# First batch by head pairs over seven PSUM banks, batch 1's q turned by TensorE, and transfers planned on one resource, in a fused attention and MLP-mixer kernel

## The chip, the cores and the metric

The kernel runs on one core of one Trainium2 chip. The metric is device time in microseconds (us). Some single runs of the kernel before fell over 1.5% above the fastest; they stand in medians and ranges, but not in ratios. A profile is one execution, and its span (first to last instruction) is some 2 us shorter than the time of the same run.

Engines: PE is TensorE (PEld its weight loads), DVE is VectorE, ACT is ScalarE, POOL is GpSimd, SP is SyncE. SPq is SP's queue, which issues the DMA transposes. POOL issues the loads. L765 is line 765 of the kernel's file; the change shifts lines, so the up products are L765 before and L779 after, the down products L859 and L874.

## The reference, cut to what matters

```python
k_proj = einsum('ks,bhsd->bhkd', E, k);  v_proj = einsum('ks,bhsd->bhkd', F, v)   # 1024 rows -> 64
attn   = softmax(q @ k_proj^T / 8)                                                # 8 batches, 8 heads, 1024 x 64
x      = (attn @ v_proj), heads side by side                                      # 1024 x 512 per batch
u      = x + (relu(x^T @ w_tok1) @ w_tok2)^T                                      # token mixing
out    = u + relu(u @ w_ch1) @ w_ch2                                              # 512 -> 1536 -> 512
```

## The kernel before

The channel product is done by a Strassen-like scheme (seven products of quarters instead of eight, for "up" and "down"). Per batch the order is: project k and v, transpose the projected k, scores, exp, attend, token mixing (all called the *front*), then u must be transposed before the up products of its two halves (j = 2b and 2b+1) can start. For batch 0 TensorE transposes u; for batches 1 to 7 a DMA transpose does it.

No engine's order is written by hand. Each piece is a job with an engine, an estimated duration and a deadline. A list scheduler in the kernel's own Python orders all jobs once, and the program is emitted and pinned in that order: **each engine's instructions stand in the planned order, whatever the real times are**.

```python
pl = Planner({"U": 3, "D": 3, "F": 2})            # banks a stream may hold; F (front) lives in banks 6 and 7
def sp(t, fn, **kw): return pl.add("SP", t, t + 2.0, fn, **kw)      # transposes and stores
def ld(mb, fn, **kw):                                               # loads: a resource of their own
    t = mb / 0.40
    return pl.add("LD", t, t + 2.0, fn, **kw)
# ... buffers that matter below
qT   = tile_of([P, H, NJ, P], BF16, "qT")
uT_t = [tile_of([P, NJ, DMC, P], BF16, f"uT{i}") for i in range(2)]   # transposed u, one per half
g21_t = [tile_of([P, 2, 2 * P], BF16, f"g21{i}") for i in range(2)]
# ... end of token2(b, si): u is turned by DMA once four row blocks are there
sp(4.0, lambda: nc.sync.dma_start_transpose(
        out=uT_t[i].rearrange("p s dc q -> p (s dc) q"),
        in_=u_t[b % 2][:, i * NJ : (i + 1) * NJ].rearrange("p s d -> p (s d)")), ...)
# ... VectorE sums of quarters of u^T, needed by four of the seven up products
def s_sums(j):
    one(0, a21, a22, add=True); one(2, a11, a21); one(1, St[:, 0], a11, deps=(0,)); one(3, a12, St[:, 1], deps=(1,))
```

The softmax here doesn't subtract the row's maximum and nothing guards it: scores larger than these inputs give would overflow.

## Time and profile before

| | |
|---|---|
| time, median of 3 runs | 475.3 us (473.65 to 480.99, the last slow) |
| span of the profiled run | 471.6 us |
| TensorE columns of the whole program, counted at 2.4 per ns | 404.3 us |
| lost against that | 67.3 us |

The "loss" is my main ruler. I add up the columns of all matmuls in the program's order (a 128x256 matmul has 256) and divide by 2400 per us: the time at which an instruction would start if TensorE never waited and took columns at that rate throughout. The trace gives when it did start; the difference is the loss up to there. The 2400 is a convention of the ruler. At a granted clock of 1.00 the trace of the kernel before has one 128x256 matmul 109 ns after the other (median, 208 to 364 us), about 2350 columns per us.

| batch whose k/v projection starts | 1 | 2 | 3 | 4 | 7 | end |
|---|---|---|---|---|---|---|
| trace, us | 57.5 | 92.8 | 152.2 | 204.1 | 360.7 | 471.6 |
| loss, us | 34.0 | 37.3 | 48.7 | 50.8 | 58.2 | 67.3 |

Three sources can be read off: 34 us in the start, 11.4 us between batches 2 and 3, and 2.2 to 2.6 us in each later batch.

Before, busy time by stretch. Columns: stretch, its length, then busy us of PE, PEld, DVE, ACT, POOL with instruction counts, granted TensorE clock, mean busy share of the DMA engines, GB/s.

```profile
core 0: us, PE busy (x) PEld busy (x) DVE busy (x) ACT busy (x) POOL busy (x), PEclk, DMA share, GB/s
0.00:52.00 52.00, 33.72 (x302) 23.25 (x304) 28.32 (x81) 13.30 (x30) 23.80 (x38) 0.74 1.17 186
104.00:156.00 52.00, 42.79 (x346) 32.91 (x348) 34.04 (x83) 23.03 (x43) 9.21 (x10) 0.93 0.67 124
208.00:260.00 52.00, 50.08 (x430) 40.02 (x432) 38.48 (x93) 28.64 (x52) 11.43 (x13) 1.00 0.72 142
```

In the first stretch TensorE is idle for a third of the time and its clock is 0.74 on average; in 104 to 156 us it is idle for 9 us; later it is nearly always busy.

Before, waits (engine and line, what was waited for: us in total, times, longest us):

```profile
PE ps L765 <- DMA uT<-u: 8.5, 1, 8.5
PE ps L464 <- DVE kp L443: 7.6, 9, 1.3
PE ps L522 <- DVE x_sb L562: 5.0, 8, 1.8
```

One single wait of 8.5 us is the largest. Before, timelines of PE, SP's queue and POOL around it (start us, us, engine, line, operation, output and input, count, idle time before and what ended it):

```profile
48.56 0.60 PE L765 MATMUL ps<-uT,wc_sb 128*128 128x256 bf16 x4
...
55.98 28.91 SPq L487 DMA_TRANSPOSE qT<-q_sb  x4
...
95.94 1.53 POOL L297 DMA_DIRECT2D k_sb<-in_k_dram  x2 [4.20 <-PE ps L596]
97.45 1.50 POOL L297 DMA_DIRECT2D v_sb<-in_v_dram  x2
...
100.52 14.79 SPq L616 DMA_TRANSPOSE uT<-u  x2
...
115.56 1.01 PE L765 MATMUL ps<-uT,wc_sb 128*128 128x256 bf16 x4 [8.49 <-DMA uT<-u]
```

The first up product starts at 48.56 us. Batch 1's transposes of u are issued from 100.52 us, just behind four loads of k and v, and the first lands 15.0 us after its issue (the chain of waits has it as one piece); 4.2 us is the shortest landing in this trace. TensorE, which has run out of batch 0's work, waits.

### The profile page before, as it was taken

What the parts mean: (1) busy time and instruction counts of PE and PEld (TensorE: products, weight loads), DVE (VectorE), ACT (ScalarE), POOL (GpSimd) and SP (SyncE); (2) the same over time, 40 slices, a digit from 0 to 9 for tenths busy, and PEclk for the clock granted to TensorE, in tenths of its full rate; (3) what the DMA queues carried; (4) which work ended last, traced back from release to release, by engine and by line L of the source; (5) the groups of instructions that cost most, each with busy time, mean ns of one, the idle gap of its engine ahead of it and who ended that gap; (6) DMA issues with size and microseconds to landing.
All of it is one profiled execution on the core that took longest, in us unless ns stands there. A gap on an engine that the chain in (4) does not pass through costs nothing.

```text
span 471.6 us, 9198 instructions
## 1 busy us (share of the span) xinstructions
PE 424.9 (90%) x3665; PEld 338.9 (72%) x3692; DVE 326.7 (69%) x784; ACT 235.3 (50%) x428; POOL 107.2 (23%) x122
## 2 busy tenths in 40 slices
PE   4757889992999989999999999999999999999994
PEld 2526768771877777878777877877777887888883
DVE  2476768681878787786957786876957796766561
ACT  1321567522563665457543764457444764455541
POOL 8541031321101412031212221040101020112112
PEclk8576999997999999999999999999999999999999
DMA  8999999979393896649742998359522402241222
GB/s 125 207 199 207 189 195 196 164 151 178 89 169 56 152 209 130 135 66 217 169 133 46 194 192 145 98 82 215 107 91 46 133 4 89 47 81 55 90 89 91
DMA packets 93675, 61.68 MB, mean 131 GB/s; under 512 B 59840, under 2 KB 89024, under 8 KB 93632
## 3 DMA queue, kind: packets, MB, share of 16 engines
q0 software_dynamic: 30784, 29.63, 40.1%
q1 hardware_dynamic: 62848, 31.46, 28.0%
q8 instruction: 29, 0.48, 0.4%
q14 instruction: 14, 0.11, 0.1%
HBM read 59.24 MB, written 16.78 MB: 161 GB/s over the span
## 4 chain that ended last, share of the span: by engine, by line
PE 63%; DVE 16%; DMA 13%; ACT 3%; issue 2%; POOL 2%; DVEq 0%; POOLq 0%; ACTq 0%
PE ps L765 23%; PE ps L859 22%; DMA uT<-u 11%; PE ps L576 5%; PE ps L596 4%; DVE S L635 3%; DVE G L799 3%; DVE x_sb L562 2%; DMA q_sb<-in_q_dram 2%; PE ps L545 2%; PE ps L427 2%; PE ps L522 2%; PE ps L653 1%; DVE G L746 1%; DVE u L607 1%
## 5 line engine op out<-in xcount | busy, mean ns | idle before, releaser
L859 PEld LDWEIGHTS <-G 128*128 128x128 bf16 x1344 | 130.8, 98 | 22.0 <-issue 1.8
L859 PE MATMUL ps<-wc_sb,G 128*128 128x256 bf16 x768 | 104.5, 273 | 1.2 <-DVE da L907 1.1
L765 PEld LDWEIGHTS <-wc_sb 128*128 128x128 bf16 x768 | 72.8, 98 | 28.4 <-issue 12.5
L786 ACT ACTIVATE G<-ps 128x512 bf16<-128x512 f32 x96 | 57.4, 597 | 62.5 <-PE ps L765 62.0
L859 PE MATMUL ps<-wT,G 128*128 128x256 bf16 x576 | 78.1, 273 | 0.1
L765 PE MATMUL ps<-uT,wc_sb 128*128 128x256 bf16 x384 | 58.0, 274 | 8.8 <-DMA uT<-u 8.5
L765 PEld LDWEIGHTS <-wT 128*128 128x128 bf16 x576 | 55.4, 98 | 14.5 <-issue 4.5
L891 POOL TENSOR_TENSOR o<-o,u 128x512 f32<-128x512 f32 x32 | 37.4, 1168 | 104.3 <-ACT o L889 104.3
L891 POOL TENSOR_TENSOR db<-db,u 128x512 f32<-128x512 f32 x16 | 19.0, 1188 | 183.6 <-ACT db L889 183.6
L765 PE MATMUL ps<-S,wc_sb 128*128 128x256 bf16 x384 | 57.6, 273 | 1.3 <-ACT ua L792 1.0
L765 PE MATMUL ps<-S,wT 128*128 128x256 bf16 x384 | 54.9, 274 | 0.0
L746 DVE CUSTOM_DVE_ANT_0 g<-ps,ub 128x512 bf16<-128x512 f32 x48 | 32.8, 684 | 30.6 <-PE ps L765 30.5
L562 DVE TENSOR_TENSOR x_sb<-ps,rdn 128x256 bf16<-128x256 f32 x128 | 50.8, 415 | 0.9
L531 ACT ACTIVATE a<-ps 128x512 bf16<-128x512 f32 x64 | 37.8, 599 | 24.9 <-PE ps L522 24.8
L792 ACT COPY ua<-ps 128x512 f32<-128x512 f32 x48 | 28.2, 587 | 38.7 <-PE ps L765 38.6
L607 DVE TENSOR_TENSOR u<-ps,x_sb 128x512 bf16<-128x512 f32 x56 | 38.0, 685 | 12.6 <-PE ps L596 12.4
L799 DVE TENSOR_TENSOR G<-G 128x512 bf16<-128x512 bf16 x96 | 44.1, 459 | 3.3
L746 DVE CUSTOM_DVE_ANT_0 G<-ps,ua 128x512 bf16<-128x512 f32 x48 | 32.8, 683 | 12.5 <-ACT ua L792 12.3
L545 PE MATMUL ps<-vb,a 128*128 128x130 bf16 x256 | 34.0, 226 | 6.2 <-DVE x_sb L562 4.7
L545 PEld LDWEIGHTS <-a 128*128 128x128 bf16 x256 | 23.5, 100 | 17.4 <-issue 10.3
L805 ACT COPY ps<-ps 128x512 f32<-128x512 f32 x48 | 28.2, 588 | 10.5 <-PE ps L765 10.1
L557 DVE RECIPROCAL rdn<-ps 128x4 f32<-128x4 f32 x128 | 21.6, 175 | 15.9 <-PE ps L545 13.8
(72 smaller groups left out, 533.1 us busy)
## 6 DMA issues: line engine op xcount, KB each, us to landing
out_dram<-o SPq DMA_DIRECT2D x32, 512.0 KB, 3.4
k_sb<-in_k_dram POOLq DMA_DIRECT2D x14, 512.0 KB, 7.3
v_sb<-in_v_dram POOLq DMA_DIRECT2D x14, 512.0 KB, 10.8
q_sb<-in_q_dram POOLq DMA_DIRECT2D x14, 512.0 KB, 7.6
wc_sb<-in_moe_w_ch_dram POOLq DMA_DIRECT2D x6, 256.0 KB, 13.0
wc_sb<-in_moe_w_ch_dram POOLq DMA_DIRECT2D x4, 384.0 KB, 12.1
k_sb<-in_k_dram POOLq DMA_DIRECT2D x4, 256.0 KB, 7.0
v_sb<-in_v_dram POOLq DMA_DIRECT2D x4, 256.0 KB, 7.6
```

What stands on the lines that cost most here:

```text
L531: lambda: nc.scalar.activation(out=a_t[h % 4], in_=bank(bk), func=ACT.Exp, scale=scale),
L545: nc.tensor.matmul(view()[:, 2 * jj : 2 * jj + 2].rearrange("p c d -> p (c d)"), a_t[h % 4][:, j * P : (j + 1) * P], vb[:, h].rearrange("k ...
L562: lambda: nc.vector.tensor_tensor(out=x_sb[:, 4 * half : 4 * half + 4, h * D : (h + 1) * D], in0=view()[:, :, 0:D], in1=rdn[:, :, None].to ...
L607: lambda: nc.vector.tensor_add(out=u_t[b % 2][:, si, :], in0=bank(bk), in1=x_sb[:, si, :]),
L746: nc.vector._custom_dve(TENSOR_ADD_SAT, out=out, in0=in0, in1=in1, s0=FMAX, s1=0.0)
L765: nc.tensor.matmul(t[:, c, :], w1_of(n, dd, 2 * m + c), a_of(j, n, dd), start=(n in (1, 7) and c == 0 and dd == 0), stop=(c == 1 and dd == 1),
L786: lambda: nc.scalar.activation(out=G[:, n, cs], in_=view(src), func=ACT.Relu),
L792: 512, lambda: nc.scalar.copy(out=dst, in_=view("y")), writes=[(name, s % 2)],
L799: 512, lambda: f(out=G[:, n, cs], in0=in0, in1=in1), ps=False, reads=deps,
L805: 512, lambda: nc.scalar.copy(out=view("y"), in_=view("x")), takes=[bk["y"]],
L859: nc.tensor.matmul(view(X_OF[n])[:, t, :], G[:, G_OF[n], cc, t * P : (t + 1) * P], w2_of(n, cc), start=(n in (1, 7) and t == 0 and cc == 0 ...
L891: 512, lambda: nc.gpsimd.tensor_add(out=dst, in0=dst, in1=u_of(sh, dh)),
```

## The change

Its intent, in order: (1) batch 0's attention uses seven PSUM banks instead of two, and runs head pair by head pair as its k, v, q land; (2) batch 1's q is transposed by TensorE, not by DMA, so that its front can start early; (3) loads, transposes and stores are planned as users of *one* resource, most by a deadline derived from who needs them; (4) the VectorE sums of weight blocks are separate jobs; (5) the planner notes whether a bank is "clean". The last point belongs to how the scheme seeds an accumulator: ScalarE copies one bank into another, and later matmuls must add to that copy. Before, four extra "blank" matmuls wrote the whole bank anew after the transposes of q; after, the planner seeds only banks whose last user wrote the whole bank. That the copy needs such a bank is the author's assumption.

```diff
-    pl = Planner({"U": 3, "D": 3, "F": 2})
+    pl = Planner(
+        {"U": 5, "D": 3, "F": 3, "S": 7},
+        {"U": range(6), "D": range(6), "F": (5, 6, 7), "S": (0, 1, 2, 3, 4, 6, 7)},
+    )
     def sp(t, fn, **kw):
-        return pl.add("SP", t, t + 2.0, fn, **kw)
+        return pl.add("DMA", t, t + 1.5, fn, **kw)
     def ld(mb, fn, **kw):
         t = mb / 0.40
-        return pl.add("LD", t, t + 2.0, fn, **kw)
+        return pl.add("DMA", t, t + 2.0, fn, **kw)
 ... loads of batch 0
-    for hp in range(HP):
-        load_heads(0, "k", 2 * hp, 2, -90 + hp)
-        load_heads(0, "v", 2 * hp, 2, -89.5 + hp)
-    for hp in range(HP):
-        load_heads(0, "q", 2 * hp, 2, -80 + hp)
+    for hp in range(HP):
+        ...
+        for name in "kvq":
+            load_heads(0, name, 2 * hp, 2, next(first))
 ... q of batch 0, after its transpose
-        pe(1, 512, lambda: blank(bank(bk)), uses=[bk], prio=due + 5)
 ... front of batch 1
+            if b == 1:
+                for hp in range(2 * i, 2 * i + 2):
+                    unit(0.4, lambda t, hp=hp: q_transpose_pe(hp, t))
-            q_transpose(begin - 15)
-            front(b + 1, begin, end)
+            if b > 0:
+                q_transpose(None)
+            front(b + 1, at - 62, at - 14)
-                    load_heads(b + 2, name, hh, H // 2, nxt - 25)
+                    load_heads(b + 2, name, hh, H // 2, None)
 (cut: the planner's clean/dirty choice of bank, longer assumed latencies, finer deadlines)
```

More of the change, by code (lines that the diff above doesn't have):

```diff
@@ L26, with __init__ @@
 class Bank:
-    def __init__(self, stream):
-        self.stream, self.jobs, self.at = stream, [], None
+    def __init__(self, stream, full=True, seeded=False):
+        self.stream, self.full, self.seeded = stream, full, seeded
+        self.jobs, self.at = [], None
         self.read, self.write = [], []
 class Planner:
-    LAG = {"PE": 0.22, "DVE": 0.10, "ACT": 0.10, "POOL": 0.15, "SP": 0.1, "LD": 0.1}
-    def __init__(self, caps):
-        self.jobs, self.caps = [], caps
+    LAG = {"PE": 0.25, "DVE": 0.15, "ACT": 0.15, "POOL": 0.2, "DMA": 0.1}
+    def __init__(self, caps, homes):
+        self.jobs, self.caps, self.homes = [], caps, homes
         self.wrote, self.readers = {}, {}
@@ L63, in add @@
                 j.deps.update(b.write)
+                j.deps.update(r for r in b.read[-1:] if r.eng != eng)
                 b.read.append(j)
@@ L93, in plan @@
         bank_free = [0.0] * 8
+        clean = [True] * 8
         held = dict.fromkeys(self.caps, 0)
@@ L105, in home @@
                 return None
-            if b.stream != "F" and turn[b.stream][0] is not b:
+            if b.stream in "UD" and turn[b.stream][0] is not b:
                 return None
             best = None
-            for i in (6, 7) if b.stream == "F" else range(6):
+            keep = [i for i in self.homes["U"] if clean[i] and bank_free[i] is not None]
+            if all(clean[:5]):
+                keep = []
+            for i in self.homes[b.stream]:
                 t = bank_free[i]
-                if t is not None and (best is None or (max(now, t), t, i) < best):
-                    best = (max(now, t), t, i)
+                if t is None or (b.seeded and not clean[i]):
+                    continue
+                if not b.seeded and clean[i] and keep and keep[-1] == keep[0] == i:
+                    continue
+                c = (max(now, t), clean[i], t, i)
+                if best is None or c < best:
+                    best = c
             return best
@@ L126, in plan @@
                             continue
-                        t, spot = h[0], h[2]
+                        t, spot = h[0], h[3]
                     cands.append((t, j.prio, j.n, j, spot))
@@ L151, in plan @@
                     bank_free[b.at] = max(x.end for x in b.jobs) + 0.1
+                    clean[b.at] = b.full
             order.append(j)
@@ L306, in load_heads @@
         )
-    ld(1.0, dma(EF[0], E), writes=["E"], prio=-100)
-    ld(0.2, dma(EF[1], F), writes=["F"], prio=-99)
+    first = iter(range(-1000, 0))
+    ld(1.0, dma(EF[0], E), writes=["E"], prio=next(first))
+    ld(0.2, dma(EF[1], F), writes=["F"], prio=next(first))
     for hp in range(HP):
-        load_heads(0, "k", 2 * hp, 2, -90 + hp)
-        load_heads(0, "v", 2 * hp, 2, -89.5 + hp)
-    for hp in range(HP):
-        load_heads(0, "q", 2 * hp, 2, -80 + hp)
-    ld(1.05, dma(wt1_sb, moe_w_tok1.rearrange("(p si) t -> p si t", p=P)), writes=["wt1"], prio=-70)
+        if hp == HP - 1:
+            w1t = moe_w_tok1.rearrange("(p si) t -> p si t", p=P)
+            ld(1.05, dma(wt1_sb, w1t), writes=["wt1"], prio=next(first))
+        for name in "kvq":
+            load_heads(0, name, 2 * hp, 2, next(first))
     w2t = moe_w_tok2.rearrange("(tc p) s -> p tc s", p=P)
-    ld(1.05, dma(wt2_sb, w2t), writes=["wt2"], prio=-69)
+    ld(1.05, dma(wt2_sb, w2t), writes=["wt2"], prio=next(first))
     w1_v = moe_w_ch1.rearrange("(dc p) (ch c) -> p dc ch c", p=P, ch=2)
@@ L327 @@
                 ),
-                writes=[("w1", m, ch)], prio=-60 + m,
+                writes=[("w1", m, ch)], prio=next(first),
             )
@@ L334 @@
                 0.786, dma(wc2_sb[:, ch, c : c + 3], w2_v[:, ch, c : c + 3]),
-                writes=[("w2", ch, c // 3)], prio=-50 + c,
+                writes=[("w2", ch, c // 3)], prio=next(first),
             )
@@ L368 @@
     for n, (src, dst) in enumerate(((EF[0], ET_sb), (EF[1], FT_sb))):
-        b = Bank("F")
+        b = Bank("F", full=False)
         def turn(src=src, b=b):
@@ L381, with combine, one @@
         dve(512, take, writes=["ET", "FT"][n : n + 1], uses=[b], prio=-150)
-    def combine(T, b11, b12, b21, b22):
-        nc.vector.tensor_sub(out=T[1], in0=b22, in1=b12)
-        nc.vector.tensor_sub(out=b12, in0=b12, in1=b11)
-        nc.vector.tensor_sub(out=T[0], in0=b22, in1=b12)
-        nc.vector.tensor_sub(out=T[2], in0=b21, in1=T[0])
-    def combine1(m):
+    def combine(T, b11, b12, b21, b22, cols, name, n, reads):
+        def one(k, out, in0, in1, *deps):
+            dve(
+                cols, lambda: nc.vector.tensor_sub(out=out, in0=in0, in1=in1), ps=False,
+                reads=reads + [(name, n, i) for i in deps], writes=[(name, n, k)],
+            )
+        one(7, T[1], b22, b12)
+        one(5, b12, b12, b11, 7)
+        one(6, T[0], b22, b12, 5)
+        one(4, T[2], b21, T[0], 6)
+    for m in range(SETS):
         cs = slice(m * cw, (m + 1) * cw)
@@ L393, in combine1 @@
             *(wc1_sb[:, dh, :, ch, cs] for dh in range(2) for ch in range(2)),
+            cols=2 * cw, name="W1", n=m, reads=[("w1", m, 0), ("w1", m, 1)],
         )
-    def combine2(c):
+    for c in range(2):
         cs = slice(3 * c, 3 * c + 3)
@@ L400, in combine2 @@
             *(wc2_sb[:, ch, cs, dh * DH : (dh + 1) * DH] for ch in range(2) for dh in range(2)),
+            cols=3 * DH, name="W2", n=c, reads=[("w2", 0, c), ("w2", 1, c)],
         )
-    for m in range(SETS):
-        pl.add(
-            "DVE", 4 * 0.34, 4 * 0.34, lambda m=m: combine1(m),
-            reads=[("w1", m, 0), ("w1", m, 1)], writes=[("W1", m)], prio=None,
-        )
-    for c in range(2):
-        pl.add(
-            "DVE", 4 * 0.5, 4 * 0.5, lambda c=c: combine2(c),
-            reads=[("w2", 0, c), ("w2", 1, c)], writes=[("W2", c)], prio=None,
-        )
+    stream = ["S"]
     def kv_proj(b, h0, hn, due):
@@ L417, in kv_proj @@
         heads = range(h0, h0 + hn)
-        bk = Bank("F")
+        bk = Bank(stream[0], full=False)
         def view():
@@ L456, in k_transpose @@
         heads = range(h0, h0 + hn)
-        bk = Bank("F")
+        bk = Bank(stream[0], full=False)
         def view():
@@ L495, in q_transpose_pe @@
     def q_transpose_pe(hp, due):
-        bk = Bank("U")
+        bk = Bank(stream[0], full=False)
         def view():
@@ L515, in q_transpose_pe @@
         )
-        pe(1, 512, lambda: blank(bank(bk)), uses=[bk], prio=due + 5)
     def scores(h, due):
-        bk = Bank("F")
+        bk = Bank(stream[0], full=False)
         pe(
@@ L535, in attend @@
     def attend(h, half, due):
-        bk = Bank("F")
+        bk = Bank(stream[0], full=False)
         rdn = rdn_t[2 * (h % 2) + half]
@@ L571, in token1 @@
     def token1(t, due):
-        bk = Bank("F")
+        bk = Bank(stream[0], full=False)
         def mm(part):
@@ L591, in token2 @@
     def token2(b, si, due):
-        bk = Bank("F")
+        bk = Bank(stream[0], full=False)
         def mm():
@@ L620, in token2 @@
                 reads=[("u", b % 2, n) for n in range(i * NJ, (i + 1) * NJ)],
-                writes=[("uT", i, n) for n in range(HP)], prio=due,
+                writes=[("uT", i, n) for n in range(HP)], prio=None,
             )
@@ L645, in token1_pair @@
         cols = slice(hp * P, (hp + 1) * P)
-        bk = Bank("F")
+        bk = Bank(stream[0], full=False)
         def view():
@@ L671, in token2_pair @@
         cols = slice(hp * P, (hp + 1) * P)
-        bk = Bank("F")
+        bk = Bank(stream[0], full=False)
         def view():
@@ L698, in u_transpose_pe @@
     def u_transpose_pe(hp, i, due):
-        bk = Bank("F")
+        bk = Bank(stream[0], full=False)
         def view():
@@ L751, in up_set @@
         cs = slice(2 * m, 2 * m + 2)
-        bk = {n: Bank("U") for n in "xyz"}
+        bk = {n: Bank("U", seeded=n == "y") for n in "xyz"}
         ub, ua, g21 = ub_t[s % 2], ua_t[s % 2], g21_t[s % 2]
@@ L774, in product @@
             ]
-            src += [("W1", m)] if n in (5, 6, 7, 4) else [("w1", m, 0 if n < 3 else 1)]
+            src += [("W1", m, n)] if n in (5, 6, 7, 4) else [("w1", m, 0 if n < 3 else 1)]
             first = n in (1, 7)
@@ L780, in product @@
                 uses=[] if first else [b], prio=due_u(s, n),
+                after=[g(i) for i in {1: (0,), 7: (2, 3, 4, 5, 6)}.get(n, ())],
             )
@@ L805, in up_set @@
             512, lambda: nc.scalar.copy(out=view("y"), in_=view("x")), takes=[bk["y"]],
-            uses=[bk["x"]],
+            uses=[bk["x"]], after=[g(1)],
         )
@@ L836, in down_block @@
         G = G_t[j % 2]
-        bk = {n: Bank("D") for n in "xyz"}
+        bk = {n: Bank("D", seeded=n == "y") for n in "xyz"}
         os = [(2 * j + sh) % 3 for sh in range(2)]
@@ L865, in product @@
         def product(n, i):
-            if n in (1, 2, 3, 5):
-                w = [("w2", {1: 0, 2: 1, 3: 1, 5: 0}[n], c) for c in range(2)]
-                w += [("W2", c) for c in range(2)] if n == 5 else []
+            if n in (1, 2, 3):
+                w = [("w2", {1: 0, 2: 1, 3: 1}[n], c) for c in range(2)]
             else:
-                w = [("W2", c) for c in range(2)]
+                w = [("W2", c, n) for c in range(2)]
             bb = bk[X_OF[n]]
@@ L922, in down_block @@
         store(1)
-    due = -60.0
     for hp in range(HP):
-        kv_proj(0, 2 * hp, 2, due + 2 * hp)
-        k_transpose(2 * hp, 2, due + 2 * hp + 1)
-    for hp in range(HP):
-        q_transpose_pe(hp, due + 8 + 2 * hp)
-        scores(2 * hp, due + 9 + 2 * hp)
-        scores(2 * hp + 1, due + 9 + 2 * hp)
+        due = -26.0 + 3.9 * hp
+        kv_proj(0, 2 * hp, 2, due)
+        k_transpose(2 * hp, 2, due + 1)
+        q_transpose_pe(hp, due + 1.5)
+        for h in (2 * hp, 2 * hp + 1):
+            scores(h, due + 2)
@@ L933 @@
         for h in (2 * hp, 2 * hp + 1):
             for half in range(2):
-                attend(h, half, due + 10 + 2 * hp)
+                attend(h, half, due + 3)
     for hp in range(HP):
-        token1_pair(hp, due + 20 + hp)
+        token1_pair(hp, -10.0 + hp)
     for i in range(2):
         for hp in range(HP):
-            token2_pair(hp, i, (due + 25 + hp) if i == 0 else 2.0 * hp + 2)
-            u_transpose_pe(hp, i, (due + 25 + hp) if i == 0 else 2.0 * hp + 3)
+            token2_pair(hp, i, (-6.0 if i == 0 else 1.0) + 0.5 * hp)
+            u_transpose_pe(hp, i, (-5.5 if i == 0 else 1.5) + 0.5 * hp)
@@ L943, in front, with unit @@
+    stream[0] = "F"
     def front(b, begin, end):
-        units = [(1.9, lambda t: kv_proj(b, 0, H, t))]
-        units.append((0.9, lambda t: k_transpose(0, H, t)))
-        units.append((0.4, lambda t: scores(0, t)))
-        units.append((0.4, lambda t: scores(1, t)))
+        units = []
+        def unit(cost, f):
+            units.append((cost, f))
+        hn = H // 2 if b == 1 else H
+        for i in range(H // hn):
+            unit(1.9 * hn / H, lambda t, i=i: kv_proj(b, i * hn, hn, t))
+            unit(0.9 * hn / H, lambda t, i=i: k_transpose(i * hn, hn, t))
+            if b == 1:
+                for hp in range(2 * i, 2 * i + 2):
+                    unit(0.4, lambda t, hp=hp: q_transpose_pe(hp, t))
+        unit(0.4, lambda t: scores(0, t))
+        unit(0.4, lambda t: scores(1, t))
@@ L948, in front @@
         for h in range(H):
             if h + 2 < H:
-                units.append((0.4, lambda t, h=h: scores(h + 2, t)))
+                unit(0.4, lambda t, h=h: scores(h + 2, t))
             for half in range(2):
-                units.append((0.25, lambda t, h=h, half=half: attend(h, half, t)))
+                unit(0.25, lambda t, h=h, half=half: attend(h, half, t))
         for n in range(TC):
-            units.append((1.8, lambda t, n=n: token1(n, t)))
+            unit(1.8, lambda t, n=n: token1(n, t))
@@ L955, in front @@
         for si in range(NSI):
-            units.append((0.55, lambda t, si=si: token2(b, si, t)))
+            unit(0.55, lambda t, si=si: token2(b, si, t))
         total = sum(c for c, _ in units)
@@ L961, in front @@
             done += c
-    for n, name in enumerate("kvq"):
-        for hh in range(0, H, H // 2):
-            load_heads(1, name, hh, H // 2, -40 + 5 * n)
+    for hh in range(0, H, H // 2):
+        for name in "kvq":
+            load_heads(1, name, hh, H // 2, next(first))
     for b in range(B):
@@ L972 @@
         if b + 1 < B:
-            begin, end = 2 * TU * (b + 1) - 62, 2 * TU * (b + 1) - 14
-            q_transpose(begin - 15)
-            front(b + 1, begin, end)
+            at = 2 * TU * (b + 1)
+            if b > 0:
+                q_transpose(None)
+            front(b + 1, at - 62, at - 14)
         if b + 2 < B:
-            nxt = 2 * TU * (b + 2) - 62
             for name in "kvq":
                 for hh in range(0, H, H // 2):
-                    load_heads(b + 2, name, hh, H // 2, nxt - 25)
+                    load_heads(b + 2, name, hh, H // 2, None)
     plan = pl.plan()
```

## The prediction

> What bounds the kernel now. From batch 2 on, TensorE is the limit: the table of busy time by stretch shows it busy 49.8 to 50.1 of every 52.0 us between 156 and 364 us. In the instruction order [...] the whole program is 404 us of matmul; the span is 471.6 us, so 67 us is lost. Laying that order against the trace, the loss has grown to 34 us when batch 1's k/v projection starts (57.5 us), 35 us at batch 2's projection (91 us), about 49 us at batch 3's (152 us), and then grows by only about 3 us per batch. Nearly everything that can be won is therefore in the first 140 us, in two places:
>
> 1. The first batch, 9 to 57 us. TensorE is busy 33.7 of the first 52 us, at a mean granted clock of 0.74 (slices at 0.50[...]). Two PSUM banks serve the attention, so scores, exp, attend, reciprocal and multiply take turns: the first up product starts at 48.6 us, though q landed by about 23 us and the channel weights by about 37 us.
> 2. The gap at 107.1 to 115.6 us: the wait list has one TensorE wait of 8.5 us for the DMA transpose of u for batch 1. Batch 1's q went through DMA transposes issued at 56.0 us, its attention came late, and u's transposes, issued at 100.5 us, landed after 15.0 us against a median of 5.3, because batch 3's k/v loads were issued at 95.9 us. [...]
>
> What the change does. Removed: four blank matmuls (0.38 us each), two DMA transposes of q. Added: 32 TensorE transposes (about 1.8 us at full clock) and four VectorE copies of 0.69 us. Moved: batch 0 runs head pair by head pair as k, v, q land; its banks go from two to seven; the VectorE weight combinations become single jobs and no longer block a reciprocal; batch 1's attention starts soon after its loads and no longer waits for SP's queue; batch 3's loads stand mostly behind u's transposes.
>
> New limits, by hand: the loads (21.5 MB by about 56 us) are unchanged, so batch 1's first half projects no earlier than about 46 us. From the last q (about 23 us), VectorE has about 25 us of work up to batch 1's first k transpose, so the loss there should be about 20 us (34 before). Little of batch 1's u wait should remain (0 to 2 us). But batch 2's attention then coincides with a run of up products without down products: about 20 us of VectorE work in 16 us of TensorE work, costing 4 to 6 us. Loss after batch 1: about 30 us instead of 49. Steady batches: the same, perhaps 1 us better each from a third front bank.
>
> Predicted: span about 451 us, time 453 us, range 442 to 466. Faster by over 2%: 0.88; within 2%: 0.11; slower: 0.01.
>
> Right if: the first up product starts at 33 to 39 us instead of 48.6; the 8.5 us wait for u is under 2 us; the period of later batches stays 51 to 52.5 us; DVE is over 90% busy in part of 25 to 50 us. Wrong if: u's transposes again meet k/v loads and take 15 us (then about 461); in-order TensorE stalls on loads slower than planned; VectorE saturation after batch 1 eats more than I allow.

The 404 us are columns at the ruler's 2400 per us. The forecast's sum: the loss after batch 1 from 49 us to about 30, later batches the same or perhaps 1 us better each, so a span of about 451 us instead of 471.6.

## The result, and the profile after

The changed kernel took 452.2 us (median of 4 runs, 449.04 to 453.87), the kernel before 475.13 us beside it. The ratio is 0.952 (95% interval 0.945 to 0.959). Ratios here are the mean time of one kernel's fast runs over that of the other's fast runs of the same rounds, so not quite the ratio of the medians. All outputs are right. The total matches the forecast. Whether the reasons do is another question.

| loss at batch | 1 | 2 | 3 | 4 | 7 | end |
|---|---|---|---|---|---|---|
| before, us | 34.0 | 37.3 | 48.7 | 50.8 | 58.2 | 67.3 |
| after, us | 20.2 | 21.3 | 22.2 | 31.6 | 37.6 | 47.0 |

The start gains 13.8 us. Part of that is clock: from 29.7 to 43.3 us the kernel before had 8.2 us of matmul at a granted clock of 0.50, which cost it by estimate half of that, 4 us; in the changed kernel the clock there was 1.00. (The half is from the changed kernel's trace: the instruction after four 128x256 up matmuls starts 0.85 us after them at a granted clock of 0.50, at 153.61 us, and 0.44 us after them at 1.00, at 143.43 us.) By batch 3 the gain is 26.5 us. Then, between batches 3 and 4, the changed kernel **loses 9.4 us where the kernel before lost 2.2**, so 7.2 us are given back.

After, busy time by stretch, same columns:

```profile
0.00:52.00 52.00, 41.40 (x452) 32.43 (x452) 34.32 (x99) 24.58 (x52) 23.82 (x38) 0.87 1.17 186
104.00:156.00 52.00, 45.49 (x384) 35.65 (x383) 38.50 (x96) 27.19 (x49) 9.10 (x10) 0.97 1.01 171
208.00:260.00 52.00, 51.22 (x447) 41.22 (x447) 40.10 (x102) 29.42 (x53) 10.65 (x13) 1.00 0.82 146
```

The first stretch holds 7.7 us more of TensorE's work. But 104 to 156 us, where the 8.5 us wait was, still has 6.5 us idle. After, waits:

```profile
PE ps L559 <- DVE x_sb L576: 9.2, 3, 6.5
PE ps L536 <- ACT kT L494: 3.7, 4, 1.1
```

The wait for u's transpose is gone from TensorE's list. In its place stands a wait of 6.5 us of an attention matmul for VectorE. After, timelines of PE, SPq, POOL and DVE, first around batch 1's transposes (90 us), then around the new wait:

```profile
36.50 0.60 PE L779 MATMUL ps<-uT,wc_sb 128*128 128x256 bf16 x4
...
90.02 5.04 SPq L630 DMA_TRANSPOSE uT<-u  x2
...
95.38 0.78 POOL L312 DMA_DIRECT2D k_sb<-in_k_dram  x1
96.15 1.50 POOL L312 DMA_DIRECT2D v_sb<-in_v_dram  x2
97.63 1.51 POOL L312 DMA_DIRECT2D q_sb<-in_q_dram  x2
...
128.82 1.53 POOL L312 DMA_DIRECT2D k_sb<-in_k_dram  x2 [3.72 <-PE ps L445]
...
136.46 0.75 POOL L312 DMA_DIRECT2D q_sb<-in_q_dram  x1
...
137.82 9.65 SPq L630 DMA_TRANSPOSE uT<-u  x1
...
152.17 0.43 DVE L649 TENSOR_TENSOR S<-uT 128x512 bf16<-128x512 bf16 x1 [6.69 <-DMA uT<-u]
...
146.39 0.60 PE L779 MATMUL ps<-uT,wc_sb 128*128 128x256 bf16 x4
153.44 0.37 PE L559 MATMUL ps<-vb,a 128*128 128x130 bf16 x2 [6.46 <-DVE x_sb L576]
153.61 1.06 PE L779 MATMUL ps<-S,wT 128*128 128x256 bf16 x4
```

Up products start at 36.5 us instead of 48.6. Batch 1's transposes are issued at 90.0 us and most of batch 3's loads stand behind them: no long landing, no wait. For batch 2 it goes the other way. Its second transpose is issued only at 137.82 us, behind batch 4's loads, and lands 14.3 us later. VectorE's next instruction in order needs that tile, so VectorE stops for 6.7 us; the attention of batch 3 behind it stops; its banks do not come free; TensorE stops. The same stall as before, two engines away from its cause. The last line shows an extra price: four up matmuls took 1.06 us right after the stall against 0.60 us before it. The granted clock, still 1.00 from 147 to 152 us while TensorE waited, was 0.50 from 152.4 to 159.2 us, with 5.8 us of matmul in it. Half of that, an estimated 2.9 us, and the wait of 6.5 us make up the 9.4 us.

### The profile page after: what moved, and what is told of

It is laid out like the page before. It is cut to its first block, busy times and chain, and to the rows that moved or that the text cites. A ratio compares the mean times of both kernels' runs of the same rounds, so it can differ in the third digit from the quotient of the medians.

```text
span 452.1 us, 9325 instructions
## 1 busy us (share of the span) xinstructions
PE 420.0 (93%) x3736; PEld 338.3 (75%) x3736; DVE 324.0 (72%) x791; ACT 235.2 (52%) x431; POOL 106.5 (24%) x122
## 3 DMA queue, kind: packets, MB, share of 16 engines
q0 software_dynamic: 30784, 29.63, 43.2%
HBM read 59.24 MB, written 16.78 MB: 168 GB/s over the span
## 4 chain that ended last, share of the span: by engine, by line
PE 71%; DVE 13%; DMA 12%; issue 2%; ACT 1%; POOL 1%; DVEq 0%; ACTq 0%; POOLq 0%
PE ps L874 26%; PE ps L779 25%; DMA uT<-u 10%; PE ps L590 5%; PE ps L610 5%; PE ps L442 3%; DVE G L814 2%; PE ps L536 2%; PE ps L559 2%; DVE S L649 2%; DMA q_sb<-in_q_dram 2%; DVE x_sb L576 1%; DVE wT L403 1%; DVE u L706 1%; PE ps L520 1%
## 5 line engine op out<-in xcount | busy, mean ns | idle before, releaser
L779 PEld LDWEIGHTS <-wc_sb 128*128 128x128 bf16 x768 | 73.3, 98 | 15.4 <-issue 2.2
L779 PE MATMUL ps<-S,wT 128*128 128x256 bf16 x384 | 56.3, 276 | 0.2 <-DVE S L649 0.2
L760 DVE CUSTOM_DVE_ANT_0 G<-ps,ua 128x512 bf16<-128x512 f32 x48 | 32.9, 685 | 16.2 <-ACT ua L807 15.4
L559 PE MATMUL ps<-vb,a 128*128 128x130 bf16 x256 | 32.0, 228 | 9.6 <-DVE x_sb L576 9.2
L807 ACT COPY ub<-ps 128x512 f32<-128x512 f32 x48 | 28.1, 586 | 21.3 <-PE ps L779 20.4
L559 PEld LDWEIGHTS <-a 128*128 128x128 bf16 x256 | 23.1, 102 | 13.6 <-issue 10.8
L610 PE MATMUL ps<-hT_sb,wt_sb 128*128 128x512 bf16 x112 | 32.6, 379 | 0.0
```

The costliest lines, as they stand in the source:

```text
L559: nc.tensor.matmul(view()[:, 2 * jj : 2 * jj + 2].rearrange("p c d -> p (c d)"), a_t[h % 4][:, j * P : (j + 1) * P], vb[:, h].rearrange("k ...
L610: nc.tensor.matmul(bank(bk), wt2_sb[:, t, si::NSI], hT_sb[:, t, :], start=(t == 0), stop=(t == TC - 1),)
L760: nc.vector._custom_dve(TENSOR_ADD_SAT, out=out, in0=in0, in1=in1, s0=FMAX, s1=0.0)
L779: nc.tensor.matmul(t[:, c, :], w1_of(n, dd, 2 * m + c), a_of(j, n, dd), start=(n in (1, 7) and c == 0 and dd == 0), stop=(c == 1 and dd == 1),
L807: 512, lambda: nc.scalar.copy(out=dst, in_=view("y")), writes=[(name, s % 2)],
```

## The experiments

All of them were planned anew by the kernel's own scheduler unless said otherwise. "Ratio" is to the kernel before, run beside it in the same rounds, because rounds and chips differ a little: its fast runs average 474.6, 475.2, 475.0 and 477.0 us in the four groups of rounds. The changed kernel's ratio is 0.952 above and 0.948 (0.943 to 0.952) in e5.

### Which part of the change earned it: e1, e2, e3, e11

**e1**: two banks for batch 0 again.

```diff
-        {"U": 5, "D": 3, "F": 3, "S": 7},
-        {..., "S": (0, 1, 2, 3, 4, 6, 7)},
+        {"U": 5, "D": 3, "F": 3, "S": 2},
+        {..., "S": (6, 7)},
```

> The changed kernel with batch 0's attention on two PSUM banks again (6 and 7), all else as changed (the plan is made anew). Theory A (the banks are what shortened the first batch): the first up product goes from 36.5 us back to 43 us or later, and the time rises by 5 to 10 us. Rival B (the order of loads and work by head pair did it, the banks hardly matter, since one head pair lands about every 4 us): first up product within 2 us of 36.5, time within 2 us of the changed kernel's 452.

468.3 us, ratio 0.985 (0.976 to 0.993). e1's first up product, from its PE timeline:

```profile
46.43 0.60 PE L779 MATMUL ps<-uT,wc_sb 128*128 128x256 bf16 x4
```

It starts at 46.4 us; loss at batch 1 32.0 us (changed kernel 20.2). Theory A holds, and is too mild: of the 13.8 us won at the start, 11.8 us hang on the banks. By batch 3 it loses another 8.9 us.

**e2**: batch 1's q by DMA transposes.

```diff
-            if b == 1:
-                for hp in range(2 * i, 2 * i + 2):
-                    unit(0.4, lambda t, hp=hp: q_transpose_pe(hp, t))
-            if b > 0:
-                q_transpose(None)
+            q_transpose(None)
```

> The changed kernel with batch 1's q turned by DMA transposes again. Theory A (TensorE transposes brought batch 1's attention, and so the transposes of u, forward): batch 1's scores start 8 us or more later, a TensorE wait on the transpose of u of 3 us or more comes back before batch 1's up products, and the time rises by 4 to 10 us. Rival B (earlier loads and planning did it): no such wait, time within 2 us of 452.

466.1 us, ratio 0.981 (0.973 to 0.988). Batch 1's first scores start at 64.8 us instead of 56.7. In e2's PE timeline two DMA waits stand where the changed kernel has none:

```profile
102.94 0.61 PE L536 MATMUL ps<-qT,kT 128*128 128x512 bf16 x1 [6.88 <-DMA qT<-q_sb]
...
114.27 1.01 PE L779 MATMUL ps<-uT,wc_sb 128*128 128x256 bf16 x4 [8.13 <-DMA uT<-u]
```

The loss jumps from 19.9 us at batch 2 to 43.8 us at batch 3 (changed kernel: 21.3 to 22.2). Theory A holds, and is too mild: the time rose by 14 us, not 4 to 10.

**e3**: loads planned on their own resource again.

```diff
     def ld(mb, fn, **kw):
-        return pl.add("DMA", t, t + 2.0, fn, **kw)
+        return pl.add("LD", t, t + 2.0, fn, **kw)
```

> The changed kernel with loads planned on a resource of their own again, so that transposes and stores are planned as if loads cost them nothing. Theory A (planning transfers on one resource keeps k and v loads away from the transposes of u): the longest landing of a transpose of u is 10 us or more before batch 1's or 2's up products, and the time rises by 3 to 8 us. Rival B (the one resource is what delays stores: a store of batch 0 stands on SP's queue for 50 us and holds the transpose of u behind it, which costs 6.5 us in batch 3): that 6.5 us wait goes and the time falls by 2 to 7 us.

469.4 us, ratio 0.988 (0.980 to 0.995). Up to batch 2 it runs like the changed kernel (loss 20.4 us); at batch 3 the loss is 37.7 us. POOL, SPq and PE timelines of e3:

```profile
87.47 0.78 POOL L312 DMA_DIRECT2D q_sb<-in_q_dram  x1 [7.29 <-DMA qT<-q_sb]
88.30 0.74 POOL L312 DMA_DIRECT2D k_sb<-in_k_dram  x1
90.17 0.79 POOL L312 DMA_DIRECT2D k_sb<-in_k_dram  x1
90.95 1.49 POOL L312 DMA_DIRECT2D v_sb<-in_v_dram  x2
...
89.09 19.12 SPq L630 DMA_TRANSPOSE uT<-u  x2
...
108.48 1.01 PE L779 MATMUL ps<-uT,wc_sb 128*128 128x256 bf16 x4 [13.64 <-DMA uT<-u]
```

This is the clearest pair. The transposes are issued within 1 us of the changed kernel's (89.1 against 90.0), but five loads go out at 87 to 92 us instead of 95 to 99. The first transpose lands after 19.4 us instead of 4.2, and TensorE waits 13.6 us. The DMA packets between its issue and its landing show what else moved: 2.78 MB of loads beside 0.55 MB of the transposes' queue. Theory A holds for this stage, though the time rose by 17 us and not by 3 to 8; rival B is refuted as the larger effect. This pair shows what loads beside a transpose cost: 15.2 us of landing.

**e11**: the load order of before (all k and v, then q), all else as changed.

```diff
-        for name in "kvq":
-            load_heads(0, name, 2 * hp, 2, next(first))
+        for name in "kv":
+            load_heads(0, name, 2 * hp, 2, next(first))
+    for hp in range(HP):
+        load_heads(0, "q", 2 * hp, 2, next(first))
```

> The changed kernel with the load order of before: all k and v, then all q, then the first token weights. Theory A (with seven banks the order hardly matters, since all of q lands at about 23 us either way and VectorE has the same work after that): first up product within 2 us of 35.5, loss at batch 1's projection within 2 us of 20, time within 1% of the changed kernel. Rival B (work by head pairs is worth nothing without loads by head pairs): first up product 40 us or later, loss at batch 1's projection 24 us or more.

449.9 us, ratio 0.943 (0.940 to 0.947); first up product 34.3 us, loss at batch 1 19.2 us. Theory A holds: loading by head pairs is worth nothing here. One of its premises was off: the last q lands at 23.0 us in e11, but at 25.7 us in the changed kernel, where it stands behind later k and v; that may be why e11 starts 2.2 us earlier (not tested).

So no part of the change alone is the gain. The banks make the start, but taking away either the TensorE transposes of q or the planning on one resource brings batch 1's stall back, at 15 to 22 us by batch 3.

### Where the 7 us went that were given back: e4 to e10, and e12

**e4**: same plan, only the stores issued from ScalarE's queue, because SP held two stores between the two transposes of batch 2's u.

```diff
-                2.0, lambda: nc.sync.dma_start(out=out_v[b, :, rows, :], in_=o_t[os[sh]]),
+                2.0, lambda: nc.scalar.dma_start(out=out_v[b, :, rows, :], in_=o_t[os[sh]]),
```

> The changed kernel, same plan, with only the output stores issued from ScalarE's queue, so that SP carries transposes alone. Theory A (the 6.5 us TensorE wait at 147 us comes from the transpose of u standing behind two stores on SP until 137.8 us): the second transpose of u for batch 2 is issued by 130 us, the wait at 147 us goes (under 1 us), and the time falls by 3 to 7 us. Rival B (the wait comes from the 14.3 us landing among k, v and q loads, not from the late issue): the transpose is issued earlier but lands 10 us or more later all the same, and TensorE still waits 3 us or more. Risk for both: ScalarE then waits in its own order for the output tiles, which would show as ScalarE waits on POOL or DVE output adds.

454.3 us, ratio 0.957 (0.949 to 0.966): not distinguishable from the changed kernel. My theory A fell. The transpose is still issued at 136.97 us and TensorE still waits 5.3 us. Nor was rival B right that it would be issued earlier. The chain of waits of e4 (start us, us, what) names what released it:

```profile
136.35 0.60 PE ps L779 x4
136.94 0.03 PE ps L559
136.97 13.20 DMA uT<-u
...
150.20 0.43 DVE S L649
```

It is an up product, the first of these lines (the 0.03 us of L559 is only the next matmul in line). There are two buffers for the transposed u, one per half, and the second half's buffer is still read by the last up product of the batch before. The order of the program, laid against the trace, agrees: that product's last matmul ends at 136.94 us, 0.03 us before the issue, while u itself had been written by 125.1 us. In the changed kernel the two times are 137.79 and 137.82 us. The stores had merely stood beside the cause.

**e5** is the changed kernel again, on the chip of e6 to e8. **e6** gives the transposed u a third buffer. That did not fit (208.66 KB per partition wanted, 207.87 there), so g21, which only VectorE writes and reads, goes from two buffers to one.

```diff
-    uT_t = [tile_of([P, NJ, DMC, P], BF16, f"uT{i}") for i in range(2)]
-    g21_t = [tile_of([P, 2, 2 * P], BF16, f"g21{i}") for i in range(2)]
+    uT_t = [tile_of([P, NJ, DMC, P], BF16, f"uT{i}") for i in range(3)]
+    g21_t = [tile_of([P, 2, 2 * P], BF16, f"g21{i}") for i in range(1)]
-                    out=uT_t[i].rearrange("p s dc q -> p (s dc) q"),
+                    out=uT_t[(2 * b + i) % 3].rearrange("p s dc q -> p (s dc) q"),
 (readers: uT_t[j % 2] becomes uT_t[j % 3])
```

**e7** keeps two buffers and plans the loads of batch b+2 only after the sums of batch b's second half, which use the transpose. **e8** does both.

```diff
-                    load_heads(b + 2, name, hh, H // 2, None)
+                    load_heads(b + 2, name, hh, H // 2, None).deps.update(pl.wrote[("S", 1, 3)])
```

> The changed kernel itself, so that the next three can be compared with it on the same chip. Every theory: within 1% of 452 us, ratio to the kernel before 0.945 to 0.96, with the TensorE wait of 5 to 7 us near 147 us.

> The changed kernel with three buffers for the transposed u instead of two (the room comes from one buffer instead of two for g21, which only VectorE writes and reads). The run with stores on ScalarE's queue showed the transpose released at 136.97 us by the last up product that reads the old buffer, not by a store. Theory A (that buffer is what issues it late): the second transpose of u for batch 2 is issued before 130 us, VectorE's wait for it (6.7 us) falls under 2 us, and the time falls by 4 to 8 us. Rival B (the k, v and q loads issued at 128 to 136 us make it land 14 us after issue): issued earlier it still meets loads, lands after 10 us or more, and the time changes by less than 3 us.

> The changed kernel with two buffers, but the loads of batch b+2 planned only after batch b's second transpose of u has been used. Theory B (loads make the transpose land late): still issued at about 137 us, it lands within 7 us instead of 14.3, VectorE's wait for it falls under 2 us, and the time falls by 4 to 8 us. Theory A (late issue alone): landing still 10 us or more, time within 3 us.

> Both: three buffers for the transposed u, and the later loads. If both causes share the wait, this is the fastest of the four, 6 to 12 us under the changed kernel, with no VectorE wait over 2 us on a transpose of u; if one cause is all, it is within 2 us of that one alone.

| | time, us | ratio to before | loss at batch 3 / 4 / 7 | longest landing of u | VectorE's waits for it |
|---|---|---|---|---|---|
| e5, changed kernel | 450.8 | 0.948 | 20.4 / 30.0 / 37.1 | 14.4 | 12.5 |
| e6, third buffer | **435.7** | 0.917 (0.914 to 0.920) | 21.2 / 21.1 / 20.6 | 5.7 | 0 |
| e7, later loads | 442.7 | 0.932 (0.929 to 0.935) | 20.8 / 25.7 / 26.1 | 9.9 | 3.8 |
| e8, both | 438.3 | 0.923 (0.920 to 0.926) | 20.0 / 20.7 / 21.4 | 5.8 | 0 |

SPq and POOL timelines, then busy time by stretch, of e6:

```profile
118.06 1.79 SPq L630 DMA_TRANSPOSE uT<-u  x1
...
124.97 2.06 SPq L630 DMA_TRANSPOSE uT<-u  x1
...
131.86 0.79 POOL L312 DMA_DIRECT2D k_sb<-in_k_dram  x1
...
104.00:156.00 52.00, 51.79 (x447) 41.19 (x449) 45.23 (x117) 30.43 (x55) 11.19 (x11) 1.00 0.97 172
208.00:260.00 52.00, 51.79 (x449) 41.89 (x452) 38.40 (x94) 30.27 (x54) 12.66 (x14) 1.00 0.83 161
```

The second transpose goes out at 124.97 us instead of about 137, before batch 4's loads (the first at 131.86 us); POOL issues no load from 120 us until it has landed, after 5.7 us, and TensorE is busy 51.8 of 52 us. The loss stays at 21 us from batch 3 to batch 7: **by the ruler, those batches cost nothing beyond their matmuls**. Both theories were half of the truth. The buffer makes the transpose late, lateness puts it among the loads, and the loads make it land late. Removing the first cause removes the second with it (15.1 us, twice what I expected); delaying only the loads leaves a late issue (8.1 us). e7 met neither theory's forecast in full: its transpose, issued at 136.56 us, still took 9.9 us to land, with one load of k issued at 134.9 us and a store beside it, and VectorE's wait fell to 3.8 us and not under 2. Doing both is 2.7 us worse than the buffer alone; why is open, since the later loads also change the plan.

**e9** is the control: two buffers for u, one for g21.

> Control for the run with three buffers: the changed kernel with two buffers for the transposed u, and only g21 cut to one buffer. If the 15 us of that run came from the third buffer, this is within 1% of the changed kernel (447 to 454 us) and keeps the wait of 5 to 7 us near 147 us. If the single g21 (another plan) did it, it is near 436 us.

449.8 us, ratio 0.945 (0.940 to 0.949), loss at batch 4 27.3 us and VectorE's waits for u 12.5 us in all. The stalls fell in other places of the plan (the longest TensorE wait is 5.2 us), but the time is the changed kernel's: the third buffer is what counts.

**e10** puts the third buffer into the kernel *before*.

> The kernel before, with three buffers for the transposed u and one for g21, nothing of the change. Theory A (the two buffers also cause the 2.4 us that every later batch of the kernel before loses, but not its 8.5 us wait of batch 1, where the buffers are long free): loss per later batch falls from 2.4 to under 1 us, the wait of 8.5 us stays at 5 us or more, the time falls by 8 to 14 us to 461 to 467. Rival B (the third buffer alone would have done all of the change's work): under 455 us.

468.3 us, ratio 0.985 (0.980 to 0.990). Its loss at batches 3, 4 and 7 is 50.0, 50.9 and 52.1 us: 0.4 to 0.5 us for each of the last batches instead of 2.4. The wait of batch 1 is untouched:

```profile
116.98 1.01 PE L765 MATMUL ps<-uT,wc_sb 128*128 128x256 bf16 x4 [8.42 <-DMA uT<-u]
```

Theory A holds in mechanism; the gain is 7 us where I had expected 8 to 14. So the 2.4 us that every batch lost in the kernel before were the two buffers as well, and the change had not touched them. The trace of the kernel before shows it: in batches 2 to 7 each second transpose goes out 0.03 us after the last reader of its buffer ends (163.99 and 164.02 us in batch 2).

**e12** adds deadlines for stores to e6.

```diff
-                reads=[o_key(sh, 0), o_key(sh, 1)], prio=None,
+                reads=[o_key(sh, 0), o_key(sh, 1)], prio=due_d(j, 16),
```

> Three buffers for the transposed u, and stores with a deadline of their own in the plan instead of none, so that no store is left for 50 us at the head of SP's queue. With the buffer free early, nothing should wait behind a store any more: within 2 us of the 435.7 us of three buffers alone. A fall of over 2 us would say that late stores still cost output tiles.

439.8 us, ratio 0.923 (0.921 to 0.926), slower than e6's 0.917. A miss: loss at batch 3 is 24.1 us instead of 21.2. The cause was not pursued; its trace has batch 1's two transposes of u landing after 8.2 and 8.8 us, against 4.4 and 4.3 in e6.

The best kernel is e6, at 435.7 us: 0.917 of the kernel before, and 15.1 us under the changed kernel on the same chip.

## Why the prediction was right or wrong, point by point

- *Time 453 us, range 442 to 466.* Measured 452.2. Right in total.
- *The start loses about 20 us instead of 34; first up product at 33 to 39 us.* 20.2 us and 36.5 us. Right, and e1 shows that the banks carry it. *DVE over 90% busy in part of 25 to 50 us*: the profile by 5 us stretches has it at 5.00 of 5 from 35 to 50 us. (The prediction put batch 2's projection before the change at 91 us with 35 us lost; the ruler above has 92.8 and 37.3.)
- *Batch 1's wait for u falls from 8.5 us to 0 to 2 us.* No TensorE wait on that transpose remains; the loss grows by 0.9 us between batches 2 and 3 instead of 11.4. Right, for both reasons given: the front starts early (e2) and batch 3's loads stand mostly behind the transposes (e3).
- *VectorE saturation in batch 2's attention costs 4 to 6 us; loss after batch 1 about 30 us.* Wrong in size. VectorE was saturated from 105 to 110 us (5.00 of 5), but TensorE was busy 5.00 of 5 in the same stretch: it had other work in order. The loss at batch 3 was 22.2 us. The forecast had counted VectorE's excess (20 us of work against 16 us of TensorE's) as a wait of TensorE. Here the engine that lagged cost the other nothing in that stretch, because the other's order held work that did not need it.
- *Steady batches the same, perhaps 1 us better.* This step failed. Batch 3, from its projection to batch 4's, took 59.1 us, not 51 to 52.5, and from batch 3 to 7 the loss grew by 15.4 us (before: 9.5). I had read the transposes of batch 1 against loads, and not asked the same of the next batch, whose second transpose must also wait for its buffer. The prediction had named this as a way to be wrong ("u's transposes again meet k/v loads and take 15 us"): it came, with 14.3 us, one batch later than meant.
- The two errors had opposite signs: the loss at batch 3 was 8 us better than forecast, and batches 3 to 7 lost about 6 to 10 us more than forecast. The total came out right partly because they cancelled, which is luck.

## What to carry to other kernels

When a stall is removed, lay the program's own matmul time against the trace, stage by stage: the total hid here that 26.5 us had been won and 7.2 given back. Here the stall was not named where it was caused: TensorE waited for VectorE, VectorE for a transfer, the transfer for a buffer that TensorE still read, and one more 4 KB buffer per partition was worth 15.1 us. Before blaming contention or queue order for a late transfer, look in the chain of waits for what released its issue.

## What else the traces show

- The same 512 KB transpose of u landed after 4.2 us at best, and after 14.3 (changed kernel), 19.4 (e3) and 21.8 us (e2) with two to five loads issued just before or after it.
- The loads read f32 and write bf16: in the kernel before, the whole program read 59.24 MB and the load queue counted 29.63 MB, half of it. The count of all queues was 205 GB/s from 9.2 to 22.8 us and 207 GB/s from 43.3 to 52.0 us, stretches full of loads, so by estimate 410 to 414 GB/s were read, with only one core at work.
- With two buffers the gap moved between VectorE and TensorE lines and batches (a TensorE wait of 6.5 us in the changed kernel, of 5.2 us elsewhere in e9), and TensorE's list of waits never named the buffer.
- The half clock came more than once: in the kernel before TensorE was busy at a granted clock of 0.50 for 9.2 us (between 9.2 and 22.8 us), 8.2 us (29.7 to 43.3) and 2.8 us (111.6 to 118.4). Half of that, an estimated 10 us or 2% of the span, was lost.
